# Reordering the opening of a fused DFT and matmul kernel: rows first, weights later, zeros on TensorE

**Chip, cores, metric.** One core of one Trainium2 chip. The metric is the device time of one execution in microseconds (us), as the median of several runs. TensorE is called PE in the profile, VectorE DVE, ScalarE ACT, GpSimd POOL, SyncE SP.

## What is computed

The input x is 8 x 3008 x 256. The kernel computes the real part of a 2D FFT over the last two axes, and then an MLP on each row. The reference, cut:

```python
X = np.fft.fft(x, axis=1)
X = np.fft.fft(X, axis=2).real          # 8 x 3008 x 256, taken as 24064 rows
h = X @ w_in                            # 256 -> 2048
g = h * np.cos(h)
out = g @ w_out                         # 2048 -> 256
```

## The kernel before

The channel FFT is folded into w_in: each quarter q of w_in is multiplied by a matrix CC and gives a quarter of `Wc` (cosine part) and `Ws` (sine part). These are the "folds", `H<-w,CC` in the profile. The FFT along the rows is done per batch by VectorE folds of four row groups (even part `E[j]`, odd part `O[j]`), followed by DFT matmuls on TensorE that fill the rings `Rr`, `Ir` and `Rb`. Then come 376 steps of the main loop. A step seeds a PSUM bank on ScalarE from `Rb` and `wex` (the last row of `Ws`), adds two matmuls P (`Rr`, `Wc`) and two Q (`Ir`, `Ws`), computes h cos h on ScalarE and VectorE, makes four sums on GpSimd, and ends with seven output matmuls that use `w2` and the sums of weights `WT`. Most of `WT` is made by accumulating transfers (DMA transfers, issued by GpSimd, that add to what is in their destination).

The opening, cut (`...` marks cuts). All is issued in this order on each engine, and the timelines below show each engine's instructions in it:

```python
zero = cpool.tile([1, 264], BF, tag="zero")      # one partition
...
for j in ORDER: load_x(0, j)                     # rows of batch 0, issued by SyncE
for g in gathers(0, ORDER): gather_x(*g)         # the other rows, by GpSimd, from table ix
spin(out=CC, ...); load_w1(0); load_mats(0); load_w1(1) ...      # SyncE
...
for _ in range(8): mm(bank("M"), zero[:, 0:128], zero[:, 0:1].to_broadcast([1, 512]), True)
fold_sin(0); turn_last(0)        # turn_last(q): 4 transfers by GpSimd, Ws -> wex[q]
fold_cos(0); warm(10)            # ten more matmuls on zeros
fold_now("c0 e0 o0 c3 e3 o3 c2 e2 o2"); add_O(2, 3)    # add_*: accumulating transfer, GpSimd
fold_now("E2"); ...; fold_now("c1 e1 E0 R0"); halve_now(0, VE[1])
fold_sin(1); turn_last(1)
first_R.early("pA", "pB"); ...; first_x.early("pC", "pD"); ...
fold_cos(1)
fold_now("o1 O0 I0"); add_O(2, 0) ...
halve_now(1, VO[1])
# then the steps, whose parts are sorted by a planned time (T is one step):
(0.95, fold_sin(2)), (2.9, fold_cos(2)), (T+0.95, fold_sin(3)), (T+2.9, fold_cos(3))
(-0.3, add_block(2, 1, 1)), (1.31, add_block(0, 0, 1)), (T+0.25, add_block(1, 0, 0))  # into WT[k]
at(-1.5 * T, load_ext)           # three loads of one channel, 4-byte elements
```

Of the kernel before, what the change touches and what calls it, by code (L numbers as in the profile page):

```python
# [19 lines left out]
ND = 256  # L20
# [98 lines left out]
def kernel(  # L119
# [45 lines left out]


    xflat = x.rearrange("b s d -> (b s) d")
    ix = cpool.tile([NP, 9], U32, tag="ix")
    nc.sync.dma_start(out=ix, in_=IX_dr.ap())
    L = [cpool.tile([128, NS * ND], FP, tag=f"xl{j}", name=f"xl{j}") for j in range(4)]  # L170

    def gather_x(b, j, a, z, n):

        pin(
            nc.gpsimd.indirect_dma_start(
                out=L[j][0:NP, a * ND : z * ND],
                out_offset=None,
                in_=xflat,
                in_offset=bass.IndirectOffsetOnAxis(ap=ix[:, n : n + 1], axis=0),
                element_offset=b * SEQ * ND,  # L180
            )
        )
# [24 lines left out]
    for j in ORDER:  # L207
        load_x(0, j)
    for g in gathers(0, ORDER):
        gather_x(*g)  # L210

    CC = cpool.tile([128, 512], FP, tag="CC")
    w1, MC = [], []
    w2 = cpool.tile([128, NF * ND], FP, tag="w2")
    WT = [
# [15 lines left out]
    def load_mats(n):  # L231
        src = MC_dr[n].ap()
        m = cpool.tile([NP, src.shape[1]], FP, tag=f"MC{n}", name=f"MC{n}")
        spin(out=m, in_=src)
        MC.append(m)
# [7 lines left out]
    spin(out=CC, in_=CC_dr.ap())  # L243
    load_w1(0)
    load_mats(0)
    load_w1(1)
    load_mats(1)
    load_w1(2)
    load_w2(0, 4)
    spin(out=WT[2][:, 2:8], in_=wout[0][:, 2:8, 128:256])  # L250
    load_w2(4, NF)
    load_w1(3)
    load_mats(2)
    spin(out=RC, in_=RC_dr.ap())
# [12 lines left out]
    Rb = cpool.tile([128, RING], FP, tag="Rb")  # L267
    R4 = cpool.tile([128, 32], FP, tag="R4")
    Rx4 = cpool.tile([128, 32], FP, tag="Rx4")
    nc.gpsimd.memset(R4, 0.0)  # L270
    nc.gpsimd.memset(Rx4, 0.0)
    zero = cpool.tile([1, 264], BF, tag="zero")
    nc.gpsimd.memset(zero, 0.0)
    r128_dr = dpool.tile([NB, HALF], FP, tag="r128", name="r128")
    r4_dr = dpool.tile([1, NB], FP, tag="r4", name="r4")

# [20 lines left out]
    def vtt(o, a, b, op):  # L297
        pin(nc.vector.tensor_tensor(out=o, in0=a, in1=b, op=op))  # L298
# [18 lines left out]
            )  # L317
        return ps

    def fold_sin(q, tag="H"):  # L320
        ps = fold_mms(q, 128, tag)
        act(Ws[:, q * 512 : (q + 1) * 512], ps)

    def turn_last(q):

        for f in range(4):
            c = q * 512 + f * 128
            pin(nc.gpsimd.dma_start(out=wex[q][:, f : f + 1], in_=Ws[127:128, c : c + 128]))

    def fold_cos(q, tag="H"):  # L330
        ps = fold_mms(q, 0, tag)
        act(Wc[:, q * 512 : (q + 1) * 512], ps)


    def sum_weights(i, k):
        v = w2.rearrange("p (q r c) -> p q r c", r=2, c=ND)[:, 2 * i : 2 * i + 2]
# [41 lines left out]
    def fold_ops():  # L378

        ops = {}  # L380
        for j in range(4):
            src = L[j][0:NP].rearrange("p (m d) -> p m d", d=ND)
            if j in (1, 2):
                src = src[:, ::-1]
            ops[f"c{j}"] = [
                (1, NS, lambda eng, c, j=j, s=src: pin(
                    eng.tensor_copy(out=VE[j][:, :, 0:1], in_=s[:, :, 0:1])
                ))
            ]
            lo, hi = src[:, :, 1:128], src[:, :, 255:128:-1]  # L390
            for key, o, op in ((f"e{j}", VE[j][:, :, 1:128], ADD), (f"o{j}", VO[j], SUB)):
                if key in ("o1", "o3"):
                    lo, hi = hi, lo
                ops[key] = [
                    (NS, 127, lambda eng, c, o=o, lo=lo, hi=hi, op=op: tto(
                        eng, o[:, c], lo[:, c], hi[:, c], op
                    ))
                ]
        for key, V, o, a, b, op in (
            ("E0", VE, 0, 0, 1, ADD),  # L400
            ("E2", VE, 2, 2, 3, ADD),
            ("R0", VE, 1, 0, 2, ADD),
            ("R1", VE, 3, 0, 2, SUB),
            ("O0", VO, 0, 0, 1, ADD),
            ("I0", VO, 1, 0, 2, SUB),
        ):
            ops[key] = [
                (NS, V[0].shape[2], lambda eng, c, V=V, o=o, a=a, b=b, op=op: tto(
                    eng, V[o][:, c], V[a][:, c], V[b][:, c], op
                ))  # L410
            ]
        return ops
# [60 lines left out]
    def fold_first():  # L473

        c = [t[0:NP].rearrange("p (m d) -> p m d", d=ND)[:, :, 128:129] for t in L]
        c[1], c[2] = c[1][:, ::-1], c[2][:, ::-1]
        a = spool.tile([128, NS], FP, tag="xa", bufs=1, name="xa")[0:NP].unsqueeze(2)
        g = spool.tile([128, NS], FP, tag="xg", bufs=1, name="xg")[0:NP].unsqueeze(2)
        vtt(a, c[0], c[1], ADD)
        vtt(g, c[2], c[3], ADD)  # L480
        vtt(a, a, g, ADD)
        z = g[:, 0:4]
        run_now(halve(a, z, 0))
        e = spool.tile([128, GW], FP, tag="G", bufs=3, name="xb")
        v = e[0:NP, 0:1280].rearrange("p (m d) -> p m d", d=128)
        act(v[:, 0:6], a[:, 0:6].to_broadcast([NP, 6, 128]))
        act(v[:, 6:10], z.to_broadcast([NP, 4, 128]))
        return lambda src, slot, n: v[0:n, 6 * src + slot]
# [47 lines left out]
    class Dft:  # L536
# [14 lines left out]
        def early(self, te, to):  # L551
            self.uv, self.pb = bank(te), bank(to)
            self.mms(0, self.uv, True)
            self.mms(1, self.pb, True)

        def copy_e(self):
            self.ab = spool.tile([128, NQ], FP, tag="ab", bufs=3, name="ab")
            act(self.ab[:, 0 : self.n], self.uv[:, 0 : self.n])
# [37 lines left out]
        def minus_sum(self):  # L596
            M = self.M
            outs = [
                (self.ring[0:M, sl], slice(1 + i, 1 + z))
                for sl, i, z in self.at_down(1, 1, NU - 2)  # L600
            ]
            if self.ri == 0:
                outs.append((R4[:, self.b : self.b + 1], slice(0, 1)))
            for o, c in outs:
                self.twice(o, c)
# [457 lines left out]

    state = {}
    total = n_tiles * 8
    for _ in range(8):
        mm(bank("M"), zero[:, 0:128], zero[:, 0:1].to_broadcast([1, 512]), True)
    sin(halfpi2)
    def warm(n):

        w = bank("M")
        for _ in range(n):
            mm(w, zero[:, 0:128], zero[:, 0:1].to_broadcast([1, 512]), True)

    fold_sin(0)
    turn_last(0)
    fold_cos(0)
    warm(10)

    def fold_now(keys):  # L1080
        for key in keys.split():
# [9 lines left out]
    add_E = lambda o, a: add_by_dma(E, o, a, NS * 128)  # L1091
    add_O = lambda o, a: add_by_dma(O, o, a, NS * 127)

    first_R, first_I = Dft(0, 0, 0, held(0, (E[1], Z[0]))), Dft(1, 0, 0)

    fold_now("c0 e0 o0 c3 e3 o3 c2 e2 o2")
    add_O(2, 3)
    fold_now("E2")
    pin(nc.vector.tensor_copy(out=L[1][0:1, 7 * ND :], in_=L[0][0:1, 0:ND]))
    fold_now("c1 e1 E0 R0")  # L1100
    halve_now(0, VE[1])
    fold_sin(1)
    turn_last(1)
    first_R.early("pA", "pB")
    first_R.copy_e()
    first_x = Dft(0, 0, 0, fold_first(), Rb, True)
    first_x.early("pC", "pD")
    first_x.copy_e()
    fold_cos(1)
    fold_now("o1 O0 I0")  # L1110
    add_O(2, 0)
    first_R.plus()
    first_x.plus()
    halve_now(1, VO[1])


    events = []
# [71 lines left out]
    def dve_room(n):  # L1189

        step, late = divmod(n, 2)
        if step < 9:
            return 0.64
        return 0.0 if step % 8 in ((1,) if late else (2, 3, 4, 5)) else 0.64

    def dve_time(n):
# [69 lines left out]
        extra.append(s)  # L1266
        return s

    def plan_dft(b, ri, kodd, n):

        d = Dft(ri, b, kodd)
        s = max((n + 1) // 2, safe(b * HALF + (kodd + 1) * RUN) - 2)
        s = bank_step(s, lambda s: b == 0 or s % 8 in (4, 5, 6, 7))
        u = (s + 2) * T
# [15 lines left out]
        return s  # L1290

    for t, fn in (
        (0.88, lambda: first_I.early("pA", "M")),
        (0.89, first_I.copy_e),
        (0.95, lambda: fold_sin(2, "pC")),
        (0.96, lambda: turn_last(2)),
        (1.0, first_I.plus),
        (2.9, lambda: fold_cos(2, "pA")),
        (T + 0.95, lambda: fold_sin(3, "pC")),
        (T + 2.9, lambda: fold_cos(3, "pA")),  # L1300
        (3 * T, lambda: turn_last(3)),
        (-0.3, lambda: add_block(2, 1, 1)),
        (1.3, lambda: less_block(0)),
        (1.31, lambda: add_block(0, 0, 1)),
        (T + 0.2, lambda: less_block(1)),
        (T + 0.25, lambda: add_block(1, 0, 0)),
    ):
        at(t, fn)
    for k in range(4):
        at(0.1, lambda k=k: sum_weights(0, k))  # L1310
    at(-1.5 * T, load_ext)
    for j in (0, 1, 2, 3):
        at(3.5 * T + 0.1, lambda j=j: load_x(1, j))
    p = pool_all(0, FOLD["R1"])
    for i in (1, 2, 3):
        on_pool(3, 0.73, lambda i=i: sum_weights(i, 3))
    p = pool_all(p, flat(twist(VE[3], 0, VZ[0])))
    g0, land = 6, [0] * 4
    for n, d in ((0, first_I), (2, first_R), (3, first_x)):
        on_dve(n, 0.5, d.minus)  # L1320
    n = dve_all(1, flat(twist(VO[2], 1, VZ[1])))
    i_step = plan_dft(0, 1, 1, n)
    for g in gathers(1, range(4)):
        land[g[1]] = g0 = on_pool(g0, 0.97, lambda g=g: gather_x(*g))
        if g[1] == 1 and g[3] == 8:
# [5 lines left out]
    at(s * T + 2.905, open_ext)  # L1331
    at(s * T + 4.75, turn_ext)
    at((s + 1) * T + 1.46, copy_ext)
    r_step = plan_dft(0, 0, 1, 2 * p + 1)
    n = 2 * s + 3
    for k in range(10):
        n = on_dve(n, 0.16, lambda k=k: fold_ext(1, k))
# [14 lines left out]
    for k in range(4):  # L1352
        n = on_dve(n, 0.2, lambda k=k: fold_ext(0, k))
    plan_ext(0, max(n, 2 * extra[-1] + 4))
    free_e, free_o = [0, 0, 0, r_step], [0, 0, i_step, 0]
    for b in range(1, NB):
        by_dve = b == 1
        free = [0] * 4
# [112 lines left out]
```

## Time and profile before

| | before |
|---|---|
| time, median of 3 runs | 1939.13 us (1939.05 to 1939.72) |
| TensorE busy | 1899.4 of 1936.3 us |
| first matmul of step 0 ("P0") | 36.90 us |
| first matmul of step 5 ("P5") | 74.21 us |
| first matmul of step 14 ("P14") | 127.45 us |

The trace shows each matmul on 4-byte operands as two records, so that a fold (two matmuls) has four. Lines from TensorE's timeline of the kernel before (start, length, what, count):

```profile
1.23 5.06 PE L292 MATMUL M<-zero 1*128 1x512 bf16 x8 [1.23 <-POOL zero L273]
...
23.35 2.34 PE L292 MATMUL M<-zero 1*128 1x512 bf16 x10
```

The same matmul on zeros starts every 0.64 us at the beginning and every 0.22 us behind the folds. Below, "warm" means full clock and "cold" half clock.

### The profile page before, as it was taken

The numbers are of one execution on the slowest core, as the hardware profiler recorded it, in microseconds if no ns is written. First come the engines' busy times: TensorE is split into PE (matmuls) and PEld (weight loads), VectorE is DVE, ScalarE is ACT, GpSimd is POOL, SyncE is SP. The second block draws the span as 40 slices with busy tenths as digits, with TensorE's granted clock in tenths as the row PEclk, the third lists the DMA queues.
The fourth block names the chain that finished last, engine by engine and source line by source line (L and its number), as shares of the span: only waits on it lengthen the run. The fifth ranks groups of instructions, "written<-read, shape, count | busy, mean of one in ns | idle before, by whom it ended". The sixth has DMA issues, their size and how long they took to land.

```text
span 1936.3 us, 28827 instructions
## 1 busy us (share of the span) xinstructions
PE 1899.4 (98%) x8951; PEld 1646.7 (85%) x8951; DVE 1450.9 (75%) x2366; ACT 1513.3 (78%) x2985; POOL 1525.5 (79%) x2054
## 2 busy tenths in 40 slices
PE   6899999999999999999999999999999999999998
PEld 3778888888888888888888888888888888888887
DVE  5788877777777777777777777777777777777777
ACT  2767888787878887888788887888878887877886
POOL 4879888898888888888889898888878676655654
PEclk9999999999999999999999999999999999999999
DMA  9724211322123112311231113311212110100101
GB/s 216 51 53 85 50 37 24 72 36 51 29 36 69 35 37 49 52 39 32 45 70 29 45 22 61 52 40 30 31 30 36 20 18 17 20 12 12 23 9 25
DMA packets 263490, 82.16 MB, mean 42 GB/s; under 512 B 240841, under 2 KB 246776, under 8 KB 263336
## 3 DMA queue, kind: packets, MB, share of 16 engines
q1 hardware_dynamic: 249240, 49.04, 14.7%
q0 software_dynamic: 11920, 31.01, 9.3%
q8 instruction: 71, 1.16, 0.3%
q14 instruction: 83, 0.68, 0.1%
q10 hardware_dynamic: 2176, 0.26, 0.1%
HBM read 38.29 MB, written 24.69 MB: 33 GB/s over the span
## 4 chain that ended last, share of the span: by engine, by line
PE 87%; ACT 5%; DVE 5%; issue 1%; POOL 1%; DMA 0%; DVEq 0%; POOLq 0%; ACTq 0%
PE H L292 34%; PE pC L292 15%; PE pD L292 15%; PE pB L292 15%; PE pA L292 8%; ACT G L304 1%; DVE G L829 1%; DVE G L298 1%; ACT M L304 1%; ACT E L304 1%; ACT z L304 1%; POOL G L301 1%; ACT H L304 0%; DVE v L298 0%; DVE M L298 0%
## 5 line engine op out<-in xcount | busy, mean ns | idle before, releaser
L301 POOL TENSOR_TENSOR G<-G 128x256 f32<-128x256 f32 x1500 | 1083.7, 734 | 349.7 <-DVE G L829 281.2
L829 DVE SCALAR_TENSOR_TENSOR G<-H,G 128x512 f32<-128x512 f32 x376 | 259.0, 689 | 225.8 <-ACT G L304 223.5
L298 DVE TENSOR_TENSOR G<-H,G 128x512 f32<-128x512 f32 x376 | 259.7, 691 | 216.5 <-ACT G L304 213.3
L292 PE MATMUL H<-Ir,Ws 127*128 127x256 f32 x1504 | 387.8, 379 | 3.8 <-ACT E L304 3.8
L292 PE MATMUL H<-Rr,Wc 128*128 128x256 f32 x1504 | 388.3, 380 | 2.8 <-ACT H L304 2.7
L292 PE MATMUL pC<-G,WT 128*128 128x256 f32 x1504 | 387.0, 379 | 0.7 <-DVE u L298 0.7
L304 ACT ACTIVATE H<-Rb,wex 128x256 f32<-128x256 f32 x752 | 360.0, 479 | 21.9 <-DVE G L829 9.6
L304 ACT ACTIVATE G<-H 128x512 int32<-128x512 f32 x376 | 223.7, 595 | 177.2 <-DVE G L298 177.2
L304 ACT ACTIVATE E<-H 128x512 f32<-128x512 f32 x376 | 223.7, 595 | 167.7 <-PE H L292 166.3
L292 PEld LDWEIGHTS H<-Ir,Ws 127*128 127x128 f32 x1504 | 283.5, 189 | 48.8 <-ACT E L304 8.5
L292 PEld LDWEIGHTS pC<-G,WT 128*128 128x128 f32 x1504 | 284.1, 189 | 43.2 <-PE H L292 1.5
L292 PEld LDWEIGHTS H<-Rr,Wc 128*128 128x128 f32 x1504 | 281.2, 190 | 43.6 <-ACT H L304 5.6
L304 ACT ACTIVATE G<-G,halfpi 128x512 f32<-128x512 f32 x376 | 269.2, 716 | 3.2 <-DVE G L298 3.0
L298 DVE TENSOR_TENSOR G<-E,H 128x512 f32<-128x512 f32 x376 | 255.1, 679 | 4.4 <-ACT Ws L304 2.5
L298 DVE TENSOR_TENSOR M<-G,M 128x512 f32<-128x512 f32 x376 | 257.5, 685 | 0.0
L829 DVE SCALAR_TENSOR_TENSOR G<-G,M 128x512 f32<-128x512 f32 x376 | 254.3, 676 | 0.5 <-ACT M L304 0.5
L304 ACT ACTIVATE M<-M,halfpi 128x512 f32<-128x512 f32 x376 | 245.2, 652 | 0.0
L292 PE MATMUL pB<-G,WT 128*128 128x256 f32 x752 | 225.4, 381 | 4.7 <-POOL G L301 4.7
L304 ACT ACTIVATE M<-G 128x512 int32<-128x512 f32 x376 | 224.1, 596 | 0.0
L292 PE MATMUL pD<-G,w 128*128 128x256 f32 x752 | 223.8, 379 | 0.1
L292 PE MATMUL pA<-G,w 128*128 128x256 f32 x752 | 223.8, 379 | 0.0
L292 PE MATMUL pB<-G,w 128*128 128x256 f32 x752 | 223.7, 379 | 0.0
(157 smaller groups left out, 2054.6 us busy)
## 6 DMA issues: line engine op xcount, KB each, us to landing
out_dram<-ot SPq DMA_DIRECT2D x496, 32.0 KB
xl<-in_x_dram SPq DMA_DIRECT2D x64, 192.0 KB
o<-o POOLq DMA_DIRECT2D x23, 381.0 KB, 4.9
e<-e POOLq DMA_DIRECT2D x21, 384.0 KB, 5.1
out_dram<-ot SPq DMA_DIRECT2D x256, 2.0 KB
Rb<-r SPq DMA_DIRECT2D x10, 376.0 KB
w<-in_moe_w_in_dram SPq DMA_DIRECT2D x4, 512.0 KB
out_dram<-ot SPq DMA_DIRECT2D x64, 28.0 KB
```

The source lines that it names most:

```text
L292: nc.tensor.matmul(out_, lhsT=lhsT, rhs=rhs, start=start, stop=stop, skip_group_check=True)
L298: pin(nc.vector.tensor_tensor(out=o, in0=a, in1=b, op=op))
L301: pin(nc.gpsimd.tensor_tensor(out=o, in0=a, in1=b, op=op))
L304: pin(nc.scalar.activation(out=o, in_=i, func=func, **kw))
L829: nc.vector.scalar_tensor_tensor(out=o, in0=h, scalar=TWO_PI, in1=c, op0=ALU.mult, op1=ALU.mult)
```

## The change

The intent: get the rows in first, move the folds of w_in from the opening into the steps, put the odd folds last, and keep TensorE busy on zeros while it waits so that its clock is up when the work comes. The diff, cut to its core:

```diff
+    ix0 = cpool.tile([NP, 2], I32, tag="ix0")
+    pin(nc.gpsimd.iota(ix0, ...))               # table of the first two gathers, no load needed
-        gather_x(*g)
+        gather_x(*g, table=None if g[1] else first_ix)
     CC = cpool.tile([128, 512], FP, tag="CC")
+    pin(nc.gpsimd.memset(CC[0:1, 0:1], 0.0))    # behind the gathers: SyncE's load of CC waits for it
...
-    for _ in range(8): mm(bank("M"), zero..., True)
-    fold_sin(0); turn_last(0); fold_cos(0); warm(10)
+    warm(52)
+    fold_mm(0, 1); fold_mm(0, 0)
-    fold_now("c0 e0 o0 c3 e3 o3 c2 e2 o2"); add_O(2, 3); fold_now("E2"); <row copy on VectorE>
-    fold_now("c1 e1 E0 R0"); halve_now(0, VE[1])
-    fold_sin(1); turn_last(1); first_R.early("pA", "pB"); ...; fold_cos(1)
+    act(<row copy>)
+    fold_now("c0 e0 o0 c3 e3 o3 c2 e2 E2 S0 c1 e1 R0"); halve_now(0, VE[3])
+    first_x = Dft(..., fold_first(), Rb, True)  # its seven small operations now on GpSimd
+    add_E(0, 1); fold_copy(0, 1); turn_last(0); fold_copy(0, 0)
+    <both DFTs, first parts, then second parts into the same banks>
-    fold_now("o1 O0 I0"); add_O(2, 0); ...; halve_now(1, VO[1])
+    fold_now("o2 O2 T0"); add_O(2, 0)
+    fold_now("o1 J0");    add_O(2, 1)
+    halve_now(1, VO[3])
...   # in the steps: six folds one by one instead of four; less_block/add_block/turn_last moved;
...   # six of the ten twist operations of E from GpSimd to VectorE
```

## The prediction

> **What bounds the kernel now.** I read, in this order: the page (busy shares and slices), who TensorE waited for, TensorE's timeline of the first 75 us, the chain of waits from 0 to 37 us, and the timelines of VectorE, ScalarE and GpSimd beside it. From the page:
>
> ```profile
> PE 1899.4 (98%) x8951; PEld 1646.7 (85%) x8951; DVE 1450.9 (75%) x2366; ACT 1513.3 (78%) x2985; POOL 1525.5 (79%) x2054
> ...
> PE   6899999999999999999999999999999999999998
> ```
>
> TensorE (PE) is busy for 98% of the span and full in every slice but the first two. So anything that lets it start its useful stream earlier moves the end by the same amount, and anything on other engines outside the opening is worth nothing unless it holds TensorE up. What it waited for, first in the first 60 us, then from 127 us to the end:
>
> ```profile
> PE H L292 <- DMA w<-in_moe_w_in_dram: 12.0, 1, 12.0
> PE pB L292 <- POOL G L301: 2.1, 1, 2.1
> PE H L292 <- ACT H L304: 1.6, 1, 1.6
> PE H L292 <- ACT E L304: 1.5, 1, 1.5
> ```
> ```profile
> PE H L292 <- ACT E L304: 2.3, 7, 0.3
> PE pB L292 <- POOL G L301: 1.3, 2, 0.8
> PE H L292 <- DVE H L706: 1.1, 1, 1.1
> PE pC L292 <- DVE u L298: 0.4, 1, 0.4
> PE H L292 <- ACT H L304: 0.3, 1, 0.3
> ```
>
> All the waits after 127 us come to 5.4 us (2.3 + 1.3 + 1.1 + 0.4 + 0.3) out of 1810: there is nothing to gain there. The opening is another matter. The first matmul of the main loop (call it P0, H<-Rr,Wc) starts at 36.90 us. The 12.0 us wait looks like the culprit, but the chain of waits says otherwise; its pieces that carry the opening:
>
> ```profile
> 8.95 7.93 DMA xl<-in_x_dram,ix
> ...
> 28.45 1.37 PE pA L292 x8
> ...
> 31.10 1.43 PE pC L292 x8
> 32.52 1.09 PE pD L292 x8
> 33.61 1.73 PE H L292 x4
> ...
> 36.90 0.48 PE H L292
> ```
>
> The sixth gather of rows lands so late that VectorE starts the third row group at 18.46; VectorE folds until 28.4; then TensorE does two DFTs (pA/pB for the real part, pC/pD for the extra channel) and a w_in fold (H, 33.61 to 35.34); ScalarE copies the fold and seeds the bank; P0. The 12.0 us wait for w_in ends at 18.27, ten us before the DFT could start anyway: it is beside the path. Only its low activity matters, through the clock:
>
> ```profile
> 38.77 1.14 PE L292 MATMUL pA<-MC,o 95*128 95x95 f32 x4 [0.74 <-issue]
> ...
> 43.11 2.90 PE L292 MATMUL pC<-w,CC 128*128 128x512 f32 x4
> ```
>
> The same four records of a fold take 1.88 us elsewhere; here 2.90. The granted clock was 0.92 from 30 to 40 us and 0.74 from 40 to 50.
>
> **What the Trainium skill says.** (1) "TensorE: Matmul & The Clock Gate", Part 1: the array's clock halves after about one idle window of 3.4 us and comes back after about as long a busy one. The trace agrees: the records show the clock at 0.5 from 38.32 to 45.15 (6.83 us), after a stretch in which TensorE sat still from 35.3 to 36.9 and again before 38.8. (2) "DMA: Bandwidth & Descriptors", section "Issuing engines are not separate DMA queues": transfers from SyncE and GpSimd share the same 16 engines and interleave. The trace agrees: gathers that take a median of 3.1 us to land over the whole run take 9.0 in the first 60 us, while the SyncE queue streams constants and weights. (3) Same page, "Anatomy of one DMA", gives a fixed cost of about 2.0 us plus bytes over 436 GB/s for a GpSimd DMA; for 192 KB that is 2.45 us, and 3.1 is what the trace shows when nothing competes.
>
> **The change part by part.**
>
> *Rows.* The two gathers of row group 0 take their table from an iota and don't wait for the small table's load (GpSimd idle 1.27 us, first gather at 2.58). The memset of zeros (0.31 us) and the iota (none in the trace; estimated at 0.3 as well) go ahead of it, so I put the first gather at 1.75, 0.8 earlier. They keep their rhythm of 1.22 us, so the eighth is issued at 10.5 to 11.4. A memset of one element of the channel matrix behind them holds back every other SyncE load from 4.90 to about 11.6. Until then only rows move: 8 x 192 KB by SyncE and 8 x 192 KB by GpSimd, 3.1 MB; at the 270 GB/s of the window from 10 to 20 us that is 11.4 us from about 2, with the last gather landing at 13.5 or so. Group 0 (second gather issued at 3.2, in company of the SyncE rows) should be there at 10 instead of 11.68, groups 3, 2 and 1 at about 10.5, 12 and 14 instead of 14.46, 18.46 and 20.4.
>
> *VectorE's chain.* From then on VectorE, not the rows, is the limit. Start-to-start times in the trace: one pair fold of 1016 elements 1.13 (1.24 when the next operation reads it), 1024 elements 1.25, a copy of column 0 0.08, the four halving operations 2.32. The new order is groups 0 and 3 with both parities (2 x 2.34), then c2 e2 E2 S0 (0.08 + 1.24 + 1.25 + 1.13), c1 e1 R0 (0.08 + 1.24 + 1.25), halving 2.32: 13.3 us. From 10.0 that ends at 23.3, where it ends at 28.4 now. Gain 5.1 us. (The removed o2 and E0 and the row copy that goes to ScalarE are 1.1 + 1.26 + 0.3 = 2.7 of it; the added S0 takes 1.2 back; the rest is rows.) The extra channel's small operations go to GpSimd, where they overlap.
>
> *TensorE up to P0.* First parts of both DFTs, then second parts into the same banks: 16 + 16 records, 2.4 us each as at 28.45 and 31.10, so 4.8 us to 28.1; ScalarE's two copies lie beside the other DFT. Then one ScalarE copy of the extra ring (0.5) and two seeds (1.0): P0 at 29.8. Between the DFTs and P0 the old kernel has a fold (1.73) and its copy (0.5); they are gone from there. So 7.1 us earlier at best. Two things can eat into this: the clock, since after 52 zero matmuls (8 took 5.06 us cold, later ones 0.22 each: they last to about 15.5) and four fold matmuls at about 17 to 20.5, TensorE sits for some 3 us again; and the first wex transfers, issued behind one accumulate at about 21 and landing 5.4 us after issue by the median, just before they are needed. I take 0.7 us for both: P0 at 30.5, a gain of 6.4.
>
> *From P0 to the fifth step after it (P5).* Now 36.90 to 74.21, 37.3 us. Work in it at warm speed: 40 records of P and Q and 42 of the products at 0.2165, an imaginary DFT 2.4, four folds 6.9, together 27.1; so 10.2 us are lost, 3 of them to the clock (the DFT took 4.4 and the first fold 2.6), the rest to waits: for the imaginary half, ScalarE's E, and GpSimd's sums (2.1 and 1.3), which stand behind 2.4 us of R1, a whole twist, and DMA issues. New: six folds instead of four, as w_in's second quarter moves in, +3.5. Against that, GpSimd gives 6 of the 10 twist operations to VectorE (some 4.3 us by the kernel's own 2.35 ns per element), and folds lie one by one in gaps instead of 2 + 2. The imaginary chain on VectorE after the real one is 8.4 us (3.6 + 2.4 + 2.4), to 31.7, when P0 and one fold (30.5 to 33.1) have just been done: that wait goes. I estimate 4.5 us lost where 10.2 are now: gain 10.2 - 4.5 - 3.5 = 2.2.
>
> *After that* the same work in the same order; 0 on average, plus or minus 1.
>
> Sum: 6.4 + 2.2 = 8.6 us. 1939.1 - 8.6 = 1930.5; as the estimate of what is lost in the steps is on the careful side, 1930.
>
> **Rivals.** (a) *The rows don't come sooner.* If gathers are slow in themselves and not from company, group 0 comes at 11 and the others as now; VectorE then ends near 26, and only about 3 us remain: 1936. For it: the first gather took 5.6 us beside rows alone. Against: 3.1 us later in the run. (b) *The weights come too late.* Everything but rows starts 6.7 us later. The channel matrix and w_in's first quarter are 0.77 MB, 2.9 us at 270 GB/s plus a fixed part: about 16.5 to 17.5, still six us ahead of the DFT. But the queue as a whole (7.72 MB in the first 60 us, 6.2 without the rows) then ends some us later too, and w_in's last quarters or a wex transfer (needed by the seeds of steps 2, 4, 6, each 5.4 us after a GpSimd queue that also waits for odd folds) can hold a step up by 2 to 3 us: 1933. (c) *The clock falls in the wait before the DFT*: 4.8 us of DFT become up to 9: 1934. (d) *It goes better*: the steps lose only 2 us and group 0 lands at 9: 1926.5. (e) More VectorE work in steps 2 to 9 makes VectorE the bound there: it was busy 18.4 of 20 us between 60 and 80. This would cost 1 to 3 us.
>
> **Range and chances.** All rivals lie between 1926 and 1936; I take 1924.5 to 1935.5 for 8 in 10. 2% is 38.8 us, more than the whole opening before P0 (36.9), so a change of over 2% is out of reach to the good; to the bad it would need a stall repeated in all 376 steps, and the main loop isn't touched. Chances: 0.01, 0.97, 0.02.
>
> **What would show it right or wrong.** VectorE's first fold at about 10 and no wait over 0.5 us in its chain to 23.3; channel matrix issued by SyncE near 11.6; P0 near 30.5; P5 near 65.5; waits of TensorE after 127 us still about 5 us in all. It is wrong if group 0 lands after 11, if P0 comes later than 33, if the clock stands at 0.5 between 20 and 35 us, or if the end gains less than P5 does, which would mean a new wait in later batches.

## More of the kernel before

P0, P5 and P14 (and P2) are read from the timeline of TensorE, as starts of the groups `H<-Rr,Wc`.

Since TensorE is full after them, they tell where a difference in time arises.

## The result, and the profile after

| | before | after |
|---|---|---|
| time, median (4 runs each) | 1939.09 us (1935.60 to 1939.72) | 1941.82 us (1939.79 to 1946.14) |
| profiled run: span | 1936.3 | 1944.0 |
| P0 | 36.90 | 36.58 |
| P5 | 74.21 | 80.28 |
| P14 | 127.45 | 135.19 |
| from P14 to the end | 1808.9 | 1808.8 |

The ratio is 1.0021, with a 95% interval of 1.0000 to 1.0041: no gain, and if anything a small loss. Ratios here are the mean time of one kernel's fast runs over that of the other's of the same rounds, so not quite the ratio of the medians quoted.

The profiled run of the changed kernel was its slowest, 4.3 us above its median, so the 7.7 us between the two profiled spans overstate the difference. They split into -0.3 at P0 (36.58 - 36.90), +6.4 from P0 to P5 (43.70 against 37.31), +1.7 from P5 to P14 (54.91 against 53.24) and nothing after.

The page after. Compare the first line with the one of before: TensorE is busier by 20 us and ends later, so much of that is no useful work.

```profile
PE 1919.2 (99%) x8986; PEld 1655.9 (85%) x8986; DVE 1449.4 (75%) x2363; ACT 1515.9 (78%) x2988; POOL 1529.8 (79%) x2057
```

What was predicted of the rows and of VectorE came true. VectorE's timeline of the changed kernel:

```profile
9.96 0.26 DVE L392 COPY e<-xl 96x8 f32<-96x8 f32 x1 [9.04 <-DMA xl<-in_x_dram,ix]
...
22.12 1.60 DVE L378 TENSOR_TENSOR e<-e 96x512 f32<-96x512 f32 x3
```

The first fold starts at 9.96 (predicted 10.0, before 11.68) and the halving ends at 23.7 (predicted 23.3, before 28.4). But the DFT doesn't start then. TensorE's timeline:

```profile
1.11 22.36 PE L298 MATMUL M<-zero 1*128 1x512 bf16 x52 [1.11 <-POOL zero L169]
23.41 6.71 PE L298 MATMUL H<-w,CC 128*128 128x512 f32 x8
...
30.37 0.68 PE L298 MATMUL pA<-MC,e 95*128 95x95 f32 x4
...
36.58 2.08 PE L298 MATMUL H<-Rr,Wc 128*128 128x256 f32 x4 [1.60 <-ACT H L310]
```

The 52 zeros take 22.36 us, 0.43 each, to the end: the clock never came up. (The eight in the kernel before were slower still, since each waits for the one before it.) The row PEclk of the page doesn't show this, it has a 9 in the first slice: the trace's clock records begin at 29.5 us, and what lies before them is printed as full clock. The zeros stand ahead of the fold in TensorE's order, and the fold's data had landed by 18.1. Then the two folds run cold, 6.71 us for the eight records that take about 3.6 us warm. The DFT waits behind it to 30.37, though its data were there at 23.7.

In the steps there are two long waits. TensorE's waits in the first 80 us of the changed kernel:

```profile
PE H L298 <- ACT H L310: 5.0, 2, 3.4
PE pB L298 <- POOL G L307: 3.4, 1, 3.4
PE M L298 <- POOL zero L169: 1.1, 1, 1.1
PE H L298 <- DVE Ir L304: 0.7, 1, 0.7
```

The chain of waits of the changed kernel says what stands behind them; each line is start, length, what:

```profile
1.11 22.36 PE M L298 x52
23.48 3.73 PE H L298 x4
27.23 0.61 ACT Ws L310
...
28.12 2.20 POOL wex L338 x4
30.32 8.58 DMA o<-o
...
40.01 13.89 DMA WT<-in_moe_w_out_dram
...
53.91 0.85 ACT WT L310
...
55.06 13.51 DMA WT<-in_moe_w_out_dram
...
68.85 0.54 POOL wex L338
```

Read it downwards. The zeros hold the first fold, the fold holds the first `wex` transfers, and those hold GpSimd's next item, the odd add `o<-o`. The second odd add accumulates into the same tile, so GpSimd waits for the first to land (8.2 us idle). Only then, at 40.0 instead of before's 34.7, does GpSimd issue the accumulate into `WT[2]`, which takes 13.9 us. ScalarE needs `WT[2]` at 49.9, waits 4.0 us in its fixed order, and so seeds step 2 late: TensorE's wait of 3.4 us. A later accumulate takes 13.5 us. The last `wex` transfer uses the same one of the eight completion semaphores that GpSimd's transfers take in turn in this trace, and waits for it, and the sums stand behind that: the other 3.4 us. Three stretches at half clock, 3.4 us each, go with the pauses (from 36.3, 56.8 and 70.5 us).

Set against the kernel before, this is less one-sided than it looks. That kernel waited too from P0 to P5, 5.7 us in four pieces (0.74, 1.52, 2.11 and 1.28) against 7.6 now, and ran 6.83 us at half clock, against some 10. At P2 the two are level (55.69 against 55.38). The loss comes from P2 to P5, 24.59 us against 18.83: two more folds (3.5 us) and two stretches at half clock, where the kernel before has none; the wait at the sum, 3.4 us, is as long as its two there (2.11 and 1.28).

### The profile page after: what moved, and what is told of

It is laid out like the page before. It is cut to its first block, busy times and chain, and to the rows that moved or that the text cites. A ratio compares the mean times of both kernels' runs of the same rounds, so it can differ in the third digit from the quotient of the medians.

```text
span 1944.0 us, 28900 instructions
## 1 busy us (share of the span) xinstructions
PE 1919.2 (99%) x8986; PEld 1655.9 (85%) x8986; DVE 1449.4 (75%) x2363; ACT 1515.9 (78%) x2988; POOL 1529.8 (79%) x2057
## 4 chain that ended last, share of the span: by engine, by line
PE 88%; ACT 4%; DVE 4%; DMA 2%; issue 1%; POOL 1%; SPq 0%; DVEq 0%; POOLq 0%
PE H L298 34%; PE pC L298 15%; PE pD L298 15%; PE pB L298 15%; PE pA L298 7%; DMA WT<-in_moe_w_out_dram 1%; ACT G L310 1%; DVE G L842 1%; PE M L298 1%; DVE G L304 1%; ACT E L310 1%; ACT z L310 1%; ACT M L310 1%; DVE v L304 1%; POOL G L307 0%
## 5 line engine op out<-in xcount | busy, mean ns | idle before, releaser
L310 ACT ACTIVATE H<-Rb,wex 128x256 f32<-128x256 f32 x752 | 359.9, 479 | 22.4 <-DVE G L842 9.6
```

The lines of the kernel that those rows point to most:

```text
L310: pin(nc.scalar.activation(out=o, in_=i, func=func, **kw))
```

## Experiments

Twelve kernels ran, five rounds each. All gave correct results. "Before" was run beside them: medians 1938.67, 1937.91 and 1937.97 in the three calls. The changed kernel was not timed again, so the comparison with it goes through the ratios to before (its own: 1.0021, 1.0000 to 1.0041). Intervals that reach over 1.0000 overlap with that; for those runs it is the traces that decide, not the times.

### 1. What held the opening: the zeros

```diff
# zeros36
-    warm(52)
+    warm(36)
# rows128
-    zero = cpool.tile([1, 264], BF, tag="zero")
+    zero = cpool.tile([128, 264], BF, tag="zero")      # and the broadcast to [128, 512]
```

> 36 zero matmuls in the opening instead of 52, nothing else. Theory A (the zeros, all 52 at the cold 0.427 us each, hold TensorE until 23.4 us, 5.3 us after w_in's first quarter landed at 18.1): the zeros end at about 16.5, the folds start at 18.2 and run cold for 6 to 7 us to about 24.7, the DFT starts at about 25 instead of 30.4 and P0 at about 31.3 instead of 36.6; but the wait of ScalarE for the accumulate into WT[2] stays, so P2 gains less than P0 (about 3.5 us), and the time is 2 to 4 us under that of the changed kernel. Rival R1 (the opening is bound by something else, say the wex transfers or the extra channel's folds on GpSimd): P0 stays within 1 us of 36.6 and the time does not move.

> The 52 zero matmuls contract over 128 rows of zeros instead of one row; same count, same columns. Theory W1 (the clock gate does not count a one-row matmul as activity, or too little of it): the clock goes to full after 3.4 to 7 us, later zeros take 0.217 us each, they end near 15 instead of 23.4, w_in's fold starts at 18.2, P0 comes at 31 or earlier. Rival W2 (zeros as data don't count, whatever the rows): still 0.427 us each to 23.4 and the time as the changed kernel's, within noise.

With 36 zeros: 1936.97 us, ratio 0.9990 (0.9975 to 1.0006); the DFT at 26.22, P0 at 32.43 (4.2 us earlier), P2 at 51.96 (3.7 earlier). Theory A holds and R1 falls. The saved time is the zeros themselves: in this run w_in landed at 19.7 and the folds still ran cold. With 52 zeros over 128 rows: 1936.15 us, ratio 0.9990 (0.9975 to 1.0005), P0 at 32.10. TensorE's timeline of that run (one of the 52 has no record):

```profile
1.13 13.22 PE L298 MATMUL M<-zero 128*128 128x512 bf16 x51 [1.13 <-POOL zero L169]
19.40 6.54 PE L298 MATMUL H<-w,CC 128*128 128x512 f32 x8 [5.05 <-DMA w<-in_moe_w_in_dram]
```

W1 holds and W2 falls: zeros of the same count and columns bring the clock up when they contract over 128 rows (51 in 13.22 us, against 52 in 22.36; full clock is recorded from 4.69 us), and do not when they contract over one. It is the height of the operand, not its data; heights between one and 128 were not tried. But then TensorE waits 5.05 us for w_in and is cold again: the clock is recorded at half from 18.34 for 6.8 us, and the folds take 6.54. The gain in time is again that the zeros end before w_in lands.

### 2. What held step 2: first attempt, a miss

```diff
# add_early (and with warm(36): both)
     turn_last(0)
+    add_block(2, 1, 1)
     fold_copy(0, 0)
...
-        (-0.2, lambda: add_block(2, 1, 1)),
```

> The accumulate into WT[2] is issued on GpSimd right behind the first wex transfers, ahead of the two odd adds, instead of behind both (40.0 us). Theory B (ScalarE waits 4.0 us for it at 49.9 and, through it, TensorE 3.4 us at P2; then GpSimd waits 3.9 us for the next accumulate at 64.9 and TensorE 3.4 us for a sum): the transfer is issued near 30.5 and lands before 45, ScalarE's wait goes, P2 comes at 52 instead of 55.7, the second wait of TensorE shrinks below 1 us, and the time falls by 5 to 7 us; P0 stays at 36.6. Rival: the odd adds then come later and their landing delays something else, so less than 2 us remain.

> 36 zeros and the early accumulate together. If theories A and B both hold, the gains add: P0 near 31.3, no wait over 1.5 us of TensorE between P0 and P5, and the time 8 to 11 us under the changed kernel's, that is 5 to 8 under the kernel before. If R1 holds it is as e3.

Early accumulate: 1944.22 us, ratio 1.0026 (1.0011 to 1.0042). Both: 1941.73, ratio 1.0016 (1.0000 to 1.0033). ScalarE's wait for `WT[2]` goes as expected (it lands at 39.9), but TensorE's wait at P2 is not 3.4 us but 8.4, and 10.5 with both:

```profile
PE H L298 <- ACT H L310: 10.0, 2, 8.4
```

The first odd add, issued at 31.2 behind `WT[2]`, now lands at 43.4. The second is issued at 44.0, and the second `wex` transfers behind it at 47.7, landing at 57.7 to 58.3; step 2's seed needs them (P2 at 58.84). So theory B as I put it was wrong: `WT[2]` was only the item that happened to stand last. What makes step 2 late is the chain of accumulating transfers in GpSimd's queue, whatever stands at its end.

### 3. The odd adds without transfers, and the zeros together with them

```diff
# odd_vector
-    fold_now("o2 O2 T0"); add_O(2, 0); fold_now("o1 J0"); add_O(2, 1)
+    fold_now("o2 O2 T0 o1 J0")
     halve_now(1, VO[3])
+    for a in (0, 1): tto(nc.vector, VO[2], VO[2], VO[a], ADD)
# rows128_76: zeros over 128 rows, and warm(76)
# best: both
```

> The two odd adds into O[2], accumulating transfers in the changed kernel, are done by VectorE (two operations of 1.2 us behind the imaginary halving, where it sits idle from 32 to 43 us). 52 zeros on one row as in the changed kernel, so P0 stays at 36.6. Theory B2 (what holds P2 is GpSimd's queue: the second odd add waits for the first one's landing, 8 us, and each accumulate takes 8 to 14 us while the single-channel loads run, so the accumulate into WT[2] or the second wex transfers come late, whichever stands behind): the accumulate into WT[2] is issued near 30.5, ScalarE no longer waits for it, P2 comes at 50 to 52 instead of 55.7, and the time is 4 to 7 us under the changed kernel's (1941.8). Rival: wex's landing alone sets P2, as in the early-accumulate run: P2 at 55 or later and no gain.

> 76 zero matmuls over 128 rows, so that warm zeros last to about 19.4, when w_in's first quarter has landed. If the clock stays full through to the folds they take 3.5 us instead of 6.7: they end at 23 and the DFT starts with VectorE's end, at 23.8; P0 at 29.9 (against 32.1 with 52 of them, and 36.6). P2 is still held by the accumulate into WT[2]: time 0 to 2 us under the 52-row-128 run's 1936.2. If P2 does not move at all the time is the same as there.

> Odd adds on VectorE and 76 zeros over 128 rows. P0 at 29.9, no wait over 2 us of TensorE between P0 and P5, P5 at 65 to 67, time 1929 to 1932, which is 7 to 10 under the kernel before: what the prediction had put down for the change itself. If wex or another landing holds P2 all the same, 1934 or more.

Odd adds on VectorE: 1933.66 us, ratio 0.9982 (0.9969 to 0.9995). P0 is unchanged (36.12), P2 comes at 51.84 instead of 55.69 and P5 at 69.91 instead of 80.28, and the clock never drops between P0 and the end of the loop. GpSimd's timeline:

```profile
30.32 1.58 POOL L357 DMA_DIRECT2D WT<-in_moe_w_out_dram  x1
...
39.90 2.21 POOL L338 DMA_DIRECT2D wex<-Ws  x4 [2.90 <-ACT Ws L310]
```

`WT[2]` is issued at 30.3 instead of 40.0 and lands at 40.5 instead of 53.9: 9.7 of these 13.4 us are the wait in the queue, 3.7 the transfer itself, with two fewer beside it. Theory B2 holds. What sets P2 now is the landing of the second `wex` transfers (50.7 to 51.9). By the ratios the gain over the changed kernel is 7.6 us, against 6.0 for 36 zeros; the two intervals overlap, and the odd adds with warm zeros, below, come to 9.3, less than the sum. So which part is the larger is not shown.

76 zeros over 128 rows: 1936.80 us, ratio 0.9992 (0.9980 to 1.0004). From TensorE's timeline:

```profile
18.98 3.59 PE L298 MATMUL H<-w,CC 128*128 128x512 f32 x8
...
32.96 2.08 PE L298 MATMUL H<-Rr,Wc 128*128 128x256 f32 x4 [5.31 <-ACT H L310]
```

The folds run warm (18.98 to 22.57) and the DFT starts at 23.05, as early as VectorE allows; yet P0 comes at 32.96, because the seed waits for `wex`: its transfers are issued at 24.3 and land at 31.0 to 32.9, right behind the even add (issued 22.1, landed 30.5). The clock then drops in that pause. So a warm opening alone buys nothing over the 52 of experiment 1.

Both: 1932.24 us, ratio 0.9973 (0.9960 to 0.9985); P0 at 32.43, P5 at 68.92. P0 missed its 29.9 for the reason just given, and P5 its 65 to 67.

### 4. Why transfers take so long there

```diff
# ext_late
-    at(-1.5 * T, load_ext)
+    at(2.5 * T, load_ext)
# ext_held: the same, and in load_ext, ahead of its loads
+        pin(nc.vector.memset(x1[0:1, 0:1], 0.0))
```

> The three loads of the single channel (4-byte elements; SyncE is on the last one from 31.0 to 52.3 us) are asked for four steps later, nothing else. Theory C (these loads are what makes the accumulates and wex land after 8 to 14 us instead of some 5): the first odd add lands near 36 instead of 38.9, the accumulate into WT[2] near 43 instead of 53.9, ScalarE's wait at P2 goes and the time falls by 3 to 6 us; or the delay only moves, to the transfers of steps 4 to 8, and the time stays. Rival: an accumulate takes 10 us of itself: landing times stay and so does the time.

> A proper test of theory C, since the last one only changed the order of issue and SyncE issued the single-channel loads at 33.6 all the same: here a one-element memset by VectorE, some way into the second step, holds them back until about 45 us or later; otherwise the changed kernel. Theory C (their 4-byte elements slow every other transfer): the first odd add, issued near 30, lands near 36 and the second within 6 us of its issue instead of 12; the accumulate into WT[2] lands by 46 instead of 53.9, and P2 comes at 50 or earlier; time 3 to 7 us under the changed kernel's 1941.8, unless the held loads do the same to the transfers of steps 2 to 6. Rival (an accumulate takes about 10 us by itself): landings as before within 2 us, time as before.

The first of these tested nothing: SyncE has no work in between, so the long single-channel load was issued at 33.6 instead of 31.0 (1941.83 us, ratio 1.0022, 1.0009 to 1.0035). In the second a memset by VectorE holds the two long loads to 54.3 and 55.0: 1934.97 us, ratio 0.9987 (0.9972 to 1.0001). GpSimd's issues from 28 to 54 us and their median time to landing, first the changed kernel, then this run:

```profile
WT<-in_moe_w_out_dram POOLq DMA_DIRECT2D x2, 384.0 KB, 13.9
o<-o POOLq DMA_DIRECT2D x2, 381.0 KB, 12.1
```
```profile
WT<-in_moe_w_out_dram POOLq DMA_DIRECT2D x3, 384.0 KB, 6.3
o<-o POOLq DMA_DIRECT2D x2, 381.0 KB, 6.6
```

The same transfers take about half as long without the 4-byte loads beside them. The second odd add, issued at 38.90, lands at 44.0 (5.1 us; 12.1 in the changed kernel), P2 comes at 49.57 instead of 55.69, and TensorE's wait there is gone. The view of the changed kernel knows one landing of each pair only, so one by one, the changed kernel first: first odd add 8.6 and 8.0 us, second 12.1 and 5.1, `WT[2]` 13.9 and 7.7. In this stretch SyncE's queue moved 12,665 packets of 4 bytes (28 to 55 us) in the changed kernel, 120 here (28 to 54). Theory C holds for what lies beside those loads. It doesn't for the first odd add, expected near 36 and landed at 38.3: its 8.0 us lie beside the weights' loads. `WT[2]` landed at 47.1, expected by 46.

### 5. Everything together

```diff
# no_add_dma: best, and E[0] += E[1] on VectorE instead of add_E(0, 1); one odd add and the
#             two minus_sum of the first DFTs moved behind the imaginary half
# all:        no_add_dma and ext_held
```

> As the best so far (76 zeros on 128 rows, odd adds on VectorE), and the even add into E[0] on VectorE too, so that no accumulate stands ahead of the first wex transfers. Theory: in the best run these landed at 31.1 to 31.9 right behind the even add (31.1), and P0 waited 4.3 us for them; now they land by 28.5 and P0 comes at 29 instead of 32.4. The second wex transfers still land late, so P2 gains 1 to 2 us only: time 1930 to 1932 against 1932.2. If wex lands at 31 anyway, it was not the add.

> The former and the held single-channel loads together. If C holds, wex for steps 2 and 3 lands within 6 us and no wait over 1 us is left between P0 and P5: P5 at 63 to 65, time 1927 to 1930. If C falls, as the former.

Without the even add's transfer: 1932.30 us, ratio 0.9974 (0.9961 to 0.9987). `wex` is issued at 23.75 and lands from 29.2, P0 comes at 30.45 (I had expected 29) and P5 at 65.95: the prediction's 30.5 and 65.5. The profiled run was the fastest of the five (1930.45). Gain against the former best: none in the median, so what P0 gained in the profiled run doesn't show clear of noise.

All: 1931.91 us (1931.24 to 1932.01), ratio 0.9971 (0.9956 to 0.9985). The held loads bring the second `wex` transfers to land within 2.0 us (9.4 in no_add_dma), but that is worth nothing here: from P0 to P5 it is 35.45 us against 35.50. P5 comes at 66.78, not at the 63 to 65 that I had expected, since P0 came later (31.33). The transfers for step 6 land late in both (54.2 to 63.3 in no_add_dma, 55.0 to 63.1 here), beside 4-byte loads in both. This is the fastest version. Its interval against the kernel before doesn't reach 1, and its upper end lies below the lower end of the changed kernel's own (1.0000); it doesn't differ clearly from the two runs before it.

### 6. The rows alone, in the kernel before

```diff
# rows_only: kernel before, with the iota table and the memset of CC[0:1, 0:1]; nothing else
```

> The kernel before with only the rows part of the change: the iota table for the first two gathers and the one-element memset that holds the other loads. Theory D (before, TensorE's own order was a second path nearly as long as VectorE's: w_in's first quarter, landing at 18.1 to 19.5 with the loads held, then two cold folds of 5 us, ten zeros 2.3, one fold 2.0): VectorE's real chain ends near 25 instead of 28.4, but the DFT can't start before 27.5 to 29; P0 moves by less than 1.5 us from 36.9, and the time stays within 2 us of before. Rival (the prediction's view, that w_in lies beside the path): DFT at 25, P0 at 33.5, time 3 us shorter.

1939.68 us, ratio 1.0010 (0.9997 to 1.0022); P0 at 37.22. VectorE's halving ends at 24.7 instead of 28.4, but TensorE's timeline of this run shows why that is worth nothing:

```profile
18.95 5.89 PE L298 MATMUL H<-w,CC 128*128 128x512 f32 x8 [12.50 <-DMA w<-in_moe_w_in_dram]
24.78 2.34 PE L298 MATMUL M<-zero 1*128 1x512 bf16 x10
27.05 1.98 PE L298 MATMUL H<-w,CC 128*128 128x512 f32 x4
28.87 0.58 PE L298 MATMUL pA<-MC,e 95*128 95x95 f32 x4
```

TensorE has its own path to the DFT, and with w_in 0.7 us later (18.95 against 18.27) it ends later than VectorE's. Theory D holds.

## Why the prediction was wrong, step by step

The prediction was 1930.0 with a range of 1924.5 to 1935.5; the result was 1941.8, outside it. The class "within 2%" was right, but that was no achievement with an opening of 37 us.

- **Rows and VectorE's chain: right.** First operation 9.96 against 10.0, end of the chain 23.7 against 23.3. Rival (a) fell.
- **"After 52 zero matmuls (8 took 5.06 us cold, later ones 0.22 each: they last to about 15.5)": the step that failed first.** I took the rate of ten zeros that ran behind four fold matmuls over 128 rows, when the clock was already up (from 21.25 us), as the rate that zeros reach by themselves. In these runs they reach it at 128 rows and not at one. They lasted to 23.5 instead of 15.5, and the folds behind them took 6.7 us instead of 3.5. In place of a gain of 6.4 at P0 there was 0.3, and with P0 after 33 one of the prediction's own signs of being wrong. Experiment 1 shows the 4.2 us of the zeros; the cold fold alone (rows128_76) is worth nothing at P0, since `wex` then takes its place.
- **"The 12.0 us wait for w_in ... is beside the path": half wrong.** It was beside the path in the kernel before, but close to it: TensorE's order (w_in, two folds, ten zeros, a third fold) ended at 27.6, 0.8 us ahead of VectorE. Bringing the rows forward alone meets it at once, as rows_only shows. The change takes the third fold out of that path, but puts 52 zeros in.
- **"I estimate 4.5 us lost where 10.2 are now": wrong, and the larger term.** From P0 to P5 the changed kernel takes 43.70 us. The work the prediction counted is 27.1 + 3.5 = 30.6, so 13.1 us are lost: 7.6 to waits (3.4 at P2, 3.4 at the sum, 0.7 for `Ir`) and some 4.8 to the clock. The latter is the sum over the groups in those stretches of what they take over the same groups at full clock: P0 0.95, the folds 0.65 and 1.6, then 0.2, 0.5 and 0.9. A gain of 2.2 was put down and a loss of 6.4 measured. I gave transfers the median of 5.4 us that `wex` had, and moved work off GpSimd by its instruction time alone. What counted in the waits was that two accumulates into one tile make GpSimd's queue wait for a landing (8.2 us), and that accumulates land after 8 to 14 us beside the single-channel loads. Rival (b) named "a GpSimd queue that also waits for odd folds", but only as 2 to 3 us, and not as this wait.
- **Rival (c), the clock in the pause before the DFT,** happened in another form: before the pause there was no warm clock to lose. With warm zeros it does fall in the pauses: in rows128 while TensorE waits for w_in (half clock from 18.3), in the run with 76 zeros in the pause before P0 (from 31.1). How long a pause it takes is open. The prediction's point (1) has the trace agree with an idle window of 3.4 us, but the pauses it names are 1.6 and 0.7 us long, and the half clock lasted 6.83. A pause of 1.6 us before P0 goes with half clock in the changed kernel (from 36.3) and with none in odd_vector.
- **"After that the same work": right.** P14 to the end 1808.8 against 1808.9. The 1.7 us between P5 and P14 in the profiled run are mainly one more stretch at half clock (128.5 to 131.9; the step from P13 takes 6.37 instead of 4.86). Rival (e), VectorE as the bound there, fell: TensorE sat idle for 2.6 us from P5 to P14, and for 2.7 before.
- **Small slips that change nothing.** 28.1 + 0.5 + 1.0 is 29.6, not 29.8; 16 x 192 KB at 270 GB/s are 11.7 us, not 11.4; the last slice of TensorE isn't full either. In point (3) the 2.45 us are an estimate from the page's formula, and 3.1 is the median of all gathers; the shortest in that trace with a known landing took 2.6.

The places that the prediction gave for P0 and P5 can be reached: no_add_dma has them at 30.45 and 65.95. But that kernel has its zeros over 128 rows and three adds on VectorE, neither of which the prediction foresaw. The times of the last two versions, 1931.9 and 1932.3, lie inside the predicted range; their gains over the kernel before, run beside them, are 5.6 and 5.0 us by the ratios (at most 8.5 and 7.6 by the intervals), less than the 8.6 of the prediction's sum.

What stays open: how much of the changed kernel's spread (1939.8 to 1946.1) is the clock. Its other runs have no trace.

## What to carry to other kernels

Work put on an in-order engine to keep it warm is a queue item like any other: check in the trace that it runs at the warm rate, and that it ends before the data it is waiting for. Before moving a transfer, ask what the engine that issues it will wait for: two accumulating transfers into one tile turned GpSimd's queue into a wait for a landing (8.2 us here), and a short operation on an idle engine may be the better add. When one path is shortened, add up the next one first, each engine in its own order.

## What the Trainium skill lacked or had wrong

- "TensorE: Matmul & The Clock Gate", Part 1, speaks of how busy TensorE is, not of the height of the operand: 52 back-to-back matmuls over one row stayed at 0.43 us for 22.4 us, well over the window of 3.4 us that the page gives for warming, while 51 over 128 rows took 13.2 us. The page's other figure, 426.7 ns for a cold matmul of 512 columns, is confirmed.
- "DMA: Bandwidth & Descriptors", "Anatomy of one DMA": 2.0 us plus bytes over 436 GB/s gives an estimate of 2.9 us for a transfer of 381 KB, and the page doesn't say that an accumulate takes longer. The accumulates of that size do: 4.7 us for the shortest landing known in any run, 4.9 by the median over the whole kernel, 8.6 and 12.1 in the changed kernel's opening. The page has no figure for what loads of single elements do to the transfers of others. Here 4-byte loads on SyncE's queue more than doubled the landing time of GpSimd's transfers (12.1 against 5.1 us for the second odd add).
- "GPSIMD Engine Reference", 3.1: the ratio of about 2 to VectorE holds for large operations (an add of 1,024 elements per partition: 2.40 us on GpSimd, 1.22 on VectorE). The extra channel's seven small ones (8 elements or fewer) took 7.3 us on GpSimd (15.6 to 22.9, 0.85 to 1.3 us each for those shown singly) and about 0.16 each on VectorE before. VectorE was busy all that time; how much of GpSimd's time comes from that is not shown.
